# Statistics, gate columns, GpSimd sums and weight loads in an attention and gated-MLP kernel

## The chip, the core and the metric

The kernel runs on one core of one Trainium2 chip. The metric is the device time of one execution in microseconds. Before the change it is 1212.62 us, the median of 8 runs (1208.95 to 1220.15).

The core has five engines that run their own instruction queues in order: TensorE (PE, with its weight loads as PEld), VectorE (DVE), ScalarE (ACT), GpSimd (POOL) and SyncE (SP, which here only issues transfers). Transfers are also issued from ACT's and POOL's queues. [...]

## What is computed

One transformer block with conditioning, on 2048 tokens of width 1024, inputs and output in bfloat16:

```python
mod = (silu(c) @ w_mod).reshape(1, 6, 1, -1)          # sa, ca, ga, sb, cb, gb
h = layernorm(x) * (1 + ca) + sa
x = x + ga * A(h)      # 32 query heads, 4 key/value heads of 128, last 512 keys of the cache, then @ wo
h = layernorm(x) * (1 + cb) + sb
x = x + gb * ((silu(h @ w_gate) * (h @ w_up)) @ w_down)      # hidden width 3584
```

## The kernel before

**Products.** Most matrix products are made with seven block products in place of eight (class `_Seven`, `gmm`, `seven_products`). For this the two operands are cut into 2x2 blocks, and sums and differences of the blocks are needed. The sums of activations are made on VectorE. The sums of weights are made once and kept: for wq on VectorE (`sum_ops` with DVE), and for wo, w_gate, w_up and w_down on GpSimd.

**GpSimd's weight units.** One unit is 128x2048 raw weights. `units` lists 16 of wo ("o"), 28 of gate and up ("g") and 14 of w_down ("d"). For each, GpSimd issues the load into a staging slot (`unit_load`, L931), makes four sums of 128x512, each in two instructions of 128x256 (`sum_ops` with parts=2, L886, for "g"; `unit_sums`, L947, for "o" and "d"), and issues the write of the four results to DRAM (`unit_write`, L954). A sum waits for the one before it. With two slots (`OFF_ST`, at 131 and 138 KB of the arena) `unit_step` issues the next unit's load after the second of the four sums; that load waits, in GpSimd's queue, until the slot's earlier write has landed. During attention two steps are placed in every five items (`unit_tick`); in the output projection there is one slot and a step at one of the four positions of a product (`o_units`).

**Stages.** First the start: columns of w_mod for sa and ca, layernorm of the first chunk of 512 tokens, first query products. Then, for each half (two chunks of 512 tokens): attention over 64 items (`attend`; an item is one head of one chunk), output projection (`o_phase`), and later the gated MLP (`gate_up` rounds, then the last product, `f_hook`). An item of `attend` issues, in this order: `pre(i)`, half of a query product, `scores(i - 1)` with ScalarE's exponentials (L784), `pv(i - 2)` with its softmax division on VectorE (L803, L806) and a transpose from SP (L809), the other half of the query product, `tick(i)`, one background step.

**Order by hand.** The order of the program is the order of the queues. At the end of each `attend`, `start_o` and `load` issue raw blocks of wo from ACT's queue (L1148) into places that overlap GpSimd's staging slots (131 to 145 KB); the tracker `T.op` makes each wait for what last used its place. In the second half this is followed, in ACT's queue, by the last items' exponentials.

**Layernorm of the second chunk.** `load_x(1)` brings the tokens (SP, L304). From item 1 on, `ln_task(1, ..., known=False)` runs as a background task, `run_bg(2)` ahead of an item's work and one step after it: for each of four tiles the statistics (`bn_stats` L414, `bn_aggr` L418, then the reciprocal root on GpSimd, L419 and L421), the normalisation (L428) and a transpose by DMA into `hT[1]` (L451); each of these transposes waits for the one before it to land, since all write the buffers of `hT[1]`. After the four tiles come eight `modulate` operations (L433). `finish` completes the task at item 9, ahead of the first query product of the second chunk, `qproj(12)`.

**Start of the attention.** `q_raw` (L660) moves query products out of PSUM, the cast at L741 takes sa, `q_bias_mm` (L668) turns it into a bias, `q_shifted` (L673) adds it and `shift` (L678) adds sa to the first chunk. The gate columns ga come from two loads of 1 MB (`load_wga`, L571, items 2 and 3) and 64 narrow matmuls (`mod_mm` at items 7, 8 and 9). `row_task` spreads a column vector into rows with ScalarE, TensorE and VectorE, for ga and for silu(c).

**MLP weights.** `take_w` (L1426, L1427) loads for one round the raw gate block, the sums of gate, the raw up block, the sums of up, in this order, from SP's queue, two rounds ahead.

Of the kernel before, what the change touches and what calls it, by code (L numbers as in the profile page):

```python
# [131 lines left out]
def bass_adaLN_cond__sliding_block_cached__swiglu_ffn__prompt_kernel(  # L132
# [130 lines left out]
    with nc.Block() as block:  # L263

        @block.gpsimd
        def _(g):
# [177 lines left out]
            def ln_task(ch, gi, ccol, cbuf, known=True):  # L444
                dst, bufs = hT[ch % 2], B_hT[ch % 2]
                for tt in range(TPC):
                    t = ch * TPC + tt
                    if not known:
                        yield from ln_stats(t)
                    norm(t, t % 8, t % 2, half=True)  # L450
                    T.op(Q_ln[t % 2], lambda: SP.dma_start_transpose(dst[:, :, tt * P:(tt + 1) * P], nscf[t % 2]),  # L451
                         reads=[B_ns4[t % 2]], writes=bufs)
                    yield
# [272 lines left out]

            qproj_mm(4, QB0[4], 0, DT)
            q_raw(4)
            mod_sa(0)
# [116 lines left out]
            class _Seven:  # L846
# [29 lines left out]
                def sum_ops(self, st, eng, parts=1):  # L876
                    r, (s1, s2, s4) = self.raw, self.s
                    R, n = self.b_raw, HK // parts
                    for (o, a, b, op, rd, wr) in ((s1, (0, P), (HK, P), ADD, [R, self.b_s3], self.b_s[0]),
                                                  (s2, s1, (0, 0), SUB, [R, self.b_s[0]], self.b_s[1]),  # L880
                                                  (s4, (HK, 0), s2, SUB, [R, self.b_s[1], self.b_s3], self.b_s[2]),
                                                  (self.s3, (0, 0), (0, P), SUB, [R], self.b_s3)):
                        for h in range(parts):
                            x, y = [r[:, z[0] + h * n:z[0] + h * n + n, z[1]:z[1] + P] if type(z) is tuple else z[:, h * n:h * n + n, :]
                                    for z in (a, b)]
                            T.op(st, lambda: eng.tensor_tensor(o[:, h * n:h * n + n, :], x, y, op), reads=rd, writes=[wr])  # L886
                        yield
# [771 lines left out]
```

The softmax here doesn't subtract the row's maximum and nothing guards it: scores larger than these inputs give would overflow.

## Time and profile before

| what | value |
|---|---|
| median of 8 runs | 1212.62 us |
| profiled execution | 1212.46 us |
| its span | 1210.7 us |
| PE busy | 1153.2 us, 95% |
| DVE busy | 738.7 us, 61% |
| ACT busy | 527.2 us, 44% |
| POOL busy | 450.1 us, 37% |
| mean granted TensorE clock | 0.982 |
| GpSimd sums L947 and L886 | 240 and 224, mean 732 and 740 ns |

The span is the time from the first to the last instruction of the profiled execution. In the lines of a timeline, the first number is the start, the second the time from the first start to the last end of the merged instructions, and the bracket at the end gives the idle time of the engine just before and what ended it. A shape is written as partitions x elements, the output before the input.

The stages as the timeline has them: start to about 34 us; attention of the first half to about 250; output projection to about 360; attention of the second half to about 600; output projection to about 697; the MLP to the end.

### The profile page before, as it was taken

The numbers are of one execution on the slowest core, as the hardware profiler recorded it, in microseconds if no ns is written. First come the engines' busy times: TensorE is split into PE (matmuls) and PEld (weight loads), VectorE is DVE, ScalarE is ACT, GpSimd is POOL, SyncE is SP. The second block draws the span as 40 slices with busy tenths as digits, with TensorE's granted clock in tenths as the row PEclk, the third lists the DMA queues.
The fourth block names the chain that finished last, engine by engine and source line by source line (L and its number), as shares of the span: only waits on it lengthen the run. The fifth ranks groups of instructions, "written<-read, shape, count | busy, mean of one in ns | idle before, by whom it ended". The sixth has DMA issues, their size and how long they took to land.

```text
span 1210.7 us, 18388 instructions
## 1 busy us (share of the span) xinstructions
PE 1153.2 (95%) x7087; PEld 588.5 (49%) x7087; DVE 738.7 (61%) x1297; ACT 527.2 (44%) x735; POOL 450.1 (37%) x655
## 2 busy tenths in 40 slices
PE   8699999999999999996299999999999999999998
PEld 5465566654446656664144444444444444444443
DVE  4756887658676766773085767545575645454535
ACT  3466777730127777884001044545301245454110
POOL 1385588503356677777614235533400000000000
PEclk9899999999999999999599999999999999999999
DMA  9869889897948999887478577676777555544453
GB/s 327 178 181 224 172 225 215 186 209 214 228 121 176 212 194 211 197 184 197 158 191 226 174 246 239 230 256 229 248 209 203 164 187 162 188 160 152 133 172 109
DMA packets 305895, 238.72 MB, mean 197 GB/s; under 512 B 132240, under 2 KB 279696, under 8 KB 305808
## 3 DMA queue, kind: packets, MB, share of 16 engines
q1 hardware_dynamic: 234800, 121.67, 42.7%
q0 software_dynamic: 16704, 60.82, 16.1%
q10 hardware_dynamic: 54304, 55.05, 14.4%
q8 instruction: 56, 0.92, 0.3%
q14 instruction: 31, 0.25, 0.1%
HBM read 172.49 MB, written 34.60 MB: 171 GB/s over the span
## 4 chain that ended last, share of the span: by engine, by line
PE 68%; DMA 16%; POOL 11%; issue 2%; DVE 2%; ACT 1%; SPq 0%; ACTq 0%; DVEq 0%; POOLq 0%
PE ps L273 68%; POOL arena L886 9%; DMA wgu_sum<-arena 6%; DMA arena<-in_B_w_gate_dram 4%; DMA arena<-in_B_w_up_dram 3%; DMA arena<-arena 1%; POOL arena L931 1%; DMA arena<-nsc 1%; DMA arena<-in_A_wq_dram 1%; POOL arena L947 0%; POOL rstd L421 0%; DVE arena L814 0%; ACT arena L784 0%; DVE st L414 0%; DVE arena L806 0%
## 5 line engine op out<-in xcount | busy, mean ns | idle before, releaser
L273 PE MATMUL ps<-arena 128*128 128x512 f16 (+2 forms) x6782 | 1145.9, 332 | 53.2 <-ACT arena L784 33.9
L273 PEld LDWEIGHTS ps<-arena 128*128 128x128 bf16 (+1 forms) x6782 | 578.3, 98 | 613.6 <-ACT arena L784 36.4
L784 ACT ACTIVATE arena<-ps 128x1024 bf16<-128x1024 f32 x256 | 261.2, 1021 | 97.6 <-PE ps L273 49.8
L817 ACT ACTIVATE tmp<-ps 128x512 f32<-128x512 f32 x166 | 99.1, 597 | 299.1 <-PE ps L273 276.9
L947 POOL TENSOR_TENSOR arena<-arena 128x256 f16<-128x256 bf16 x240 | 174.4, 732 | 85.3 <-DMA arena<-in_B_w_down_dram 62.4
L886 POOL TENSOR_TENSOR arena<-arena 128x256 f16<-128x256 bf16 x224 | 165.7, 740 | 66.4 <-DMA arena<-in_B_w_up_dram 26.3
L814 DVE TENSOR_TENSOR arena<-ps,tmp 128x512 bf16<-128x512 f32 (+1 forms) x134 | 91.7, 684 | 51.8 <-PE ps L273 45.0
L803 DVE RECIPROCAL rl<-ps 128x4 f32<-128x4 f32 x128 | 23.0, 180 | 137.0 <-PE ps L273 136.9
L814 DVE TENSOR_TENSOR arena<-ps,nsc 128x512 f16<-128x512 f32 x84 | 57.8, 688 | 79.9 <-PE ps L273 68.2
L817 ACT ACTIVATE nsc<-ps 128x512 f32<-128x512 f32 x84 | 50.1, 597 | 95.7 <-PE ps L273 93.2
L806 DVE TENSOR_TENSOR arena<-ps,rl 128x512 f16<-128x512 f32 x128 | 88.4, 691 | 5.1 <-DMA arena<-arena 0.7
L1043 DVE TENSOR_TENSOR arena<-arena 128x2048 f16<-128x2048 f16 (+3 forms) x56 | 58.3, 1052 | 12.3 <-PE ps L273 11.7
L1493 ACT ACTIVATE arena<-arena 128x512 f16<-128x512 f16 x84 | 49.8, 624 | 30.5 <-DVE arena L814 30.5
L886 DVE TENSOR_TENSOR arena<-arena 128x512 f16<-128x512 bf16 x104 | 57.2, 550 | 1.0 <-DMA arena<-in_A_wq_dram 0.9
L814 DVE TENSOR_TENSOR tmp<-ps,tmp 128x512 f32<-128x512 f32 x32 | 22.1, 690 | 52.8 <-ACT tmp L817 43.9
L817 ACT ACTIVATE arena<-ps 128x512 f32<-128x512 f32 x16 | 9.6, 597 | 93.9 <-PE ps L273 93.9
L414 DVE BATCH_NORM_STATS2 st<-x_res 128x6 f32<-128x512 bf16 x62 | 42.3, 682 | 3.9 <-DMA x_res<-in_A_x_dram 3.4
L1510 DVE TENSOR_TENSOR arena<-ps,arena 128x512 f16<-128x512 f32 x28 | 19.4, 691 | 37.1 <-PE ps L273 37.1
L931 POOL DMA_DIRECT2D arena<-in_B_w_down_dram x14 | 11.0, 786 | 72.3 <-DMA wd_sum<-arena 44.1
L1111 DVE TENSOR_TENSOR tmp<-tmp,rowb 128x512 f32<-128x512 f32 x48 | 34.5, 720 | 1.6
L931 POOL DMA_DIRECT2D arena<-in_B_w_gate_dram x14 | 13.1, 935 | 58.7 <-PE ps L273 44.3
L1508 DVE TENSOR_TENSOR arena<-arena 128x512 f16<-128x512 f16 x84 | 34.7, 438 | 0.3
(85 smaller groups left out, 434.6 us busy)
## 6 DMA issues: line engine op xcount, KB each, us to landing
arena<-wgu_sum SPq DMA_DIRECT2D x56, 512.0 KB, 6.9
arena<-in_A_wq_dram SPq DMA_DIRECT2D x28, 512.0 KB, 5.0
wgu_sum<-arena POOLq DMA_DIRECT2D x28, 512.0 KB, 4.6
arena<-wo_sum ACTq DMA_DIRECT2D x7, 2048.0 KB, 9.3
arena<-in_B_w_gate_dram SPq DMA_DIRECT2D x28, 512.0 KB, 4.2
arena<-in_B_w_up_dram SPq DMA_DIRECT2D x28, 512.0 KB, 7.0
arena<-wd_sum ACTq DMA_DIRECT2D x8, 1792.0 KB, 8.1
arena<-in_B_w_down_dram ACTq DMA_DIRECT2D x6, 1792.0 KB, 7.3
```

The costliest lines, as they stand in the source:

```text
L273: T.op(PE, lambda: TE.matmul(out_ap, lhsT, rhs, start=start, stop=stop, skip_group_check=skip), reads=reads, writes=[bank_buf])
L414: T.op(DVE, lambda: V.bn_stats(st_[sl][:, hf * 6:hf * 6 + 6], x_res[:, t, hf * 512:hf * 512 + 512]), reads=[B_x[t]], writes=[B_st[sl]])
L784: T.op(ACT, lambda: A.activation(ex_s[es][:, 2 * kp:2 * kp + 2, :], banks2(SCB + 2 * kp), AF.Exp, scale=att_scale), writes=[PB[SCB + 2 * k ...
L806: T.op(DVE, lambda: V.tensor_tensor(o_s[os_].rearrange("p (a b) d -> p a b d", a=2), psap(PVB * 512, [[512, 2], [130, 2], [1, P]]), rlb, A ...
L814: T.op(DVE, lambda: V.tensor_tensor(out, bank(ba), other, ADD), reads=[ob2], writes=[PB[ba], ob])
L817: T.op(ACT, lambda: A.activation(dst, bank(bk), AF.Copy), writes=[PB[bk], db])
L886: T.op(st, lambda: eng.tensor_tensor(o[:, h * n:h * n + n, :], x, y, op), reads=rd, writes=[wr])
L931: T.op(Q_of[slot][0], lambda: g.dma_start(dst, src), writes=[w.b_raw, w.b_s3])
L947: T.op(POOL, lambda: g.tensor_tensor(o[:, c], a[:, c], b[:, c], SUB), reads=rd, writes=[wr])
L1043: T.op(DVE, lambda: V.tensor_tensor(o, a, b, SUB), reads=rd, writes=[sb])
L1493: T.op(ACT, lambda: A.activation(o, s_, AF.Silu), reads=[sb], writes=[ob])
L1508: T.op(DVE, lambda: V.tensor_tensor(gu[blk][:, p, :], o, s_, MULT), reads=[sb, ob], writes=[B_gu[blk][p]])
```

## The change

There are four edits.

1. Second chunk. `load_x(1)` is issued ahead of the first load of v and the second of k. The statistics of its first two tiles are made ahead of the attention, after the fifth query product has left PSUM (`stats_now`), those of the third and fourth in items 2 and 3. Each tile is normalised and transposed (`norm_turn`) in items 1 to 4, and the eight modulations come in items 7 and 8, four each, in the item's own order and no longer as a background task.
2. Gate columns. Their loads move from items 2 and 3 to 7 and 8, their matmuls from items 7, 8, 9 to 12, 13, 14. The row of silu(c) is made from item 5 on, the row of ga from item 14 on. Two blocks of the attention output are taken into use at item 14 and not 12.
3. GpSimd makes each of a unit's four sums with one instruction of 128x512.
4. `take_w` issues both raw loads ahead of both loads of sums.

```diff
             for k2 in range(DT // 2):
                 load_wsa(k2)
+            load_x(1)
             load_v(0)
             load_k(1)
-            load_x(1)
...
+            def norm_turn(ch, tt):
+                t = ch * TPC + tt
+                norm(t, t % 8, t % 2, half=True)
+                T.op(Q_ln[t % 2], lambda: SP.dma_start_transpose(hT[ch % 2][:, :, tt * P:(tt + 1) * P], nscf[t % 2]),
+                     reads=[B_ns4[t % 2]], writes=B_hT[ch % 2])
...
+            def stats_now(t):
+                for _ in ln_stats(t):
+                    pass
+
             qproj_mm(4, QB0[4], 0, DT)
             q_raw(4)
+            stats_now(TPC)
+            stats_now(TPC + 1)
             mod_sa(0)
...
-                        for h in range(parts):
...
-                            T.op(st, lambda: eng.tensor_tensor(o[:, h * n:h * n + n, :], x, y, op), reads=rd, writes=[wr])
+                        T.op(st, lambda: eng.tensor_tensor(o, a, b, op), reads=rd, writes=[wr])
...
-                    yield from w.sum_ops(POOL, g, 2)
+                    yield from w.sum_ops(POOL, g)
...
-                    for h in range(2):
-                        c = slice(256 * h, 256 * h + 256)
-                        T.op(POOL, lambda: g.tensor_tensor(o[:, c], a[:, c], b[:, c], SUB), reads=rd, writes=[wr])
+                    T.op(POOL, lambda: g.tensor_tensor(o, a, b, SUB), reads=rd, writes=[wr])
...
-                if i in (2, 3):
-                    load_wga(i - 2)
+                if i in (7, 8):
+                    load_wga(i - 7)
...
                 if i == 1:
-                    late["ln"] = ln_task(1, 0, 0, B_mode, known=False)
-                    bg.append(late["ln"])
                     scores(0)
-                if i < 9:
-                    run_bg(2)
...
-                    if i + 3 == ND:
-                        finish(late["ln"])
                     qproj(i + 3)
-                for k in {7: (0, 1, 2, 3), 8: (4, 5), 9: (6, 7)}.get(i, ()):
+                if i < 5:
+                    norm_turn(1, i - 1)
+                if 1 < i < 4:
+                    stats_now(TPC + i)
+                if i in (7, 8):
+                    for dt in range(4 * (i - 7), 4 * (i - 7) + 4):
+                        modulate(hT[1], B_hT[1], dt, 0, 0, B_mode)
+                if i == 5:
+                    bgx.append(row_task(sc_row, B_scr, sc_bf[:, :], B_sc))
+                for k in {12: (0, 1, 2), 13: (3, 4, 5), 14: (6, 7)}.get(i, ()):
                     mod_mm(wga[:, k, :], B_wga[k], k, GCOLS)
...
-                        bgx.append(row_task(sc_row, B_scr, sc_bf[:, :], B_sc))
-                if i == ND:
+                if i == ND + 2:
                     take_oT(2)
                     take_oT(3)
...
                     T.op(Q_w[sl][m][0], lambda: SP.dma_start(w.raw, src), writes=[w.b_raw])
+                for m, w in enumerate(W_of[q]):
                     T.op(Q_w[sl][m][1], lambda: SP.dma_start(w.four, wgu_sum[p, m]), reads=[B_uw[("g", p, m)]], writes=[w.b_s3] + w.b_s)
```

More of the change, by code (lines that the diff above doesn't have):

```diff
@@ L442, in ln_stats, with ln_task @@
                 yield
-            def ln_task(ch, gi, ccol, cbuf, known=True):
+            def norm_turn(ch, tt):
[3 more added lines that the diff above has]
+                     reads=[B_ns4[t % 2]], writes=B_hT[ch % 2])
+            def ln_task(ch, gi, ccol, cbuf):
                 dst, bufs = hT[ch % 2], B_hT[ch % 2]
                 for tt in range(TPC):
[L447 to L452, printed above, removed]
+                    norm_turn(ch, tt)
                     yield
@@ L874, in sums, with sum_ops @@
                         pass
[L876 to L882, printed above, removed]
[L883 to L886 removed]
+                def sum_ops(self, st, eng):
+                    r, (s1, s2, s4), s3 = self.raw, self.s, self.s3
+                    R = self.b_raw
+                    a11, a12 = r[:, 0:HK, 0:P], r[:, HK:DT, 0:P]
+                    a21, a22 = r[:, 0:HK, P:2 * P], r[:, HK:DT, P:2 * P]
+                    for (o, a, b, op, rd, wr) in ((s1, a21, a22, ADD, [R, self.b_s3], self.b_s[0]),
+                                                  (s2, s1, a11, SUB, [R, self.b_s[0]], self.b_s[1]),
+                                                  (s4, a12, s2, SUB, [R, self.b_s[1], self.b_s3], self.b_s[2]),
+                                                  (s3, a11, a21, SUB, [R], self.b_s3)):
+                        T.op(st, lambda: eng.tensor_tensor(o, a, b, op), reads=rd, writes=[wr])
                         yield
```

## The prediction

> **What bounds the kernel now.** I read the page's busy shares, then who TensorE waits for, then the timeline around its longest wait, then the first 70 us. TensorE is busy 1153.2 of 1210.7 us, so at most 57 us can go without less work. Its waits, columns total us, times, longest us:
>
> ```profile
> PE ps L273 <- ACT arena L784: 33.9, 4, 32.4
> PE ps L273 <- DVE arena L806: 5.6, 1, 5.6
> PE ps L273 <- DVE bq L668: 3.6, 2, 2.5
> ```
>
> One wait, 32.4 us, is over half of what is idle. It lies where the second attention pass ends:
>
> ```profile
> 558.57 7.60 PE L273 MATMUL ps<-arena 128*128 128x512 bf16 x58 [0.51 <-ACT arena L784]
> 584.50 0.58 POOL L954 DMA_DIRECT2D wgu_sum<-arena  x1 [0.30 <-POOL arena L886]
> 585.99 5.75 POOL L947 TENSOR_TENSOR arena<-arena 128x256 f16<-128x256 bf16 x8
> 587.55 8.81 ACTq L1148 DMA_DIRECT2D arena<-in_A_wo_dram  x3
> 592.04 0.65 POOL L954 DMA_DIRECT2D wd_sum<-arena  x1 [0.30 <-POOL arena L947]
> 596.41 2.14 ACT L784 ACTIVATE arena<-ps 128x1024 bf16<-128x1024 f32 x2 [35.87 <-POOL rstd L419]
> 598.61 13.66 PE L273 MATMUL ps<-arena 128*128 128x129 bf16 x63 [32.45 <-ACT arena L784]
> ```
>
> ScalarE holds a softmax exponential that TensorE needs, but ahead of it in ScalarE's queue are loads of wo (L1148) into the staging slots in which GpSimd forms weight sums. The first is issued when the write of 584.50 has landed (3.0 us), the last when that of 592.04 has (595.04). So GpSimd's weight units end 29 us after TensorE stops (566.2), and TensorE's end moves with them. The label "rstd" is merely what GpSimd ran last. The chain of waits agrees: from 280.0 to 595 it holds GpSimd sums, their writes and loads; before 280.0 it holds TensorE, whose products free the first slot (GpSimd's load of 280.00 waited 44.31 us for them). A unit's cycle in the two-slot stage:
>
> ```profile
> 450.44 2.90 POOL L886 TENSOR_TENSOR arena<-arena 128x256 f16<-128x256 bf16 x4 [1.70 <-DMA arena<-in_B_w_gate_dram]
> 455.82 0.94 POOL L931 DMA_DIRECT2D arena<-in_B_w_up_dram  x1 [2.49 <-DMA wgu_sum<-arena]
> 456.78 2.99 POOL L886 TENSOR_TENSOR arena<-arena 128x256 f16<-128x256 bf16 x4
> 460.08 0.58 POOL L954 DMA_DIRECT2D wgu_sum<-arena  x1 [0.31 <-POOL arena L886]
> 460.76 2.90 POOL L886 TENSOR_TENSOR arena<-arena 128x256 f16<-128x256 bf16 x4
> ```
>
> Four sums, wait for the other slot's write, load, four sums, write. Here both DMA waits show, so only one of the two halves counts in a cycle. The mean cycle from 387.87 to 584.50 is 9.83 us, of which 7.9 is GpSimd's own.
>
> The front, where the second chunk's layernorm is made:
>
> ```profile
> 26.87 0.69 DVE L660 COPY arena<-ps 128x512 f32<-128x512 f32 x1 [4.19 <-PE ps L273]
> 27.48 0.15 DVE L741 CAST mod_bf<-ps 128x8 bf16<-128x8 f32 x1
> 31.77 1.41 DVE L414 BATCH_NORM_STATS2 st<-x_res 128x6 f32<-128x512 bf16 x2
> 33.60 5.34 PE L273 MATMUL ps<-arena 128*128 128x512 f16 x28 [2.52 <-DVE bq L668]
> 55.94 2.82 DVE L433 TENSOR_SCALAR arena<-arena,gain,mod_bf 128x512 f16<-128x512 f16 x4 [5.18 <-DMA arena<-nsc]
> 60.23 4.78 PE L273 MATMUL ps<-arena 128*128 128x129 bf16 x24 [5.63 <-DVE arena L806]
> ```
>
> VectorE stands 5.18 us at the modulation (L433) until the last of four serial transposes lands; item 4's softmax division (L806) is behind it, and TensorE behind that.
>
> [...] Here 128x256 takes 0.669 us at the median (0.655 least); no 128x512 is shown. [...] VectorE's L886 sums take 0.412 to 0.910 us, GpSimd's up to 1.729. [...] Here v's first group, k's second and x's second chunk land at 26.2, 26.6 and 29.3 us, in order of issue.
>
> **The change, part by part.** The sum is made against the profiled execution: 1212.46 us, span 1210.7 and 1.8 around it; the median of eight is 1212.62.
>
> *GpSimd sums whole.* Eight instructions a unit become four. A pair now takes 2 x 0.745 = 1.49 us start to start. [...] Saved 0.20 a pair, 0.40 a half unit. Lower end: no fixed part, 1.34 + 0.07, 0.08 a pair[...]. Upper: if all of the 128x1 scalar operation's 0.22 us (L419) is fixed, 512 takes 1.12 and 0.30 is saved.
> How many halves count: I replayed GpSimd's own instructions from 280 to 595 with the landing time of each load and write as it was. In the single-slot stage (five units, 288 to 373) both halves count, 10; of the following 21 two-slot units one, 21; in the final units, where TensorE stands and DMA is fast (cycles 8.4 to 8.8), both, 5 more. 36 halves x 0.40 = 14.4 us. Bounds: 36 x 0.16 = 6 and 36 x 0.60 = 22. Further, from 288 to 342 the eight sums took 9.88, 7.23 and 8.18 us instead of 6.0, because VectorE's big subtractions alternate with them: 7.3 us lost; with half as many instructions perhaps half the waits: +3. DMA is busy 0.96 to 1.01 in 375 to 500; units 4% closer together may lengthen landings: 0.1 us on some 26 cycles, -2. Sum -15 on the end of the units, and as 15 is under 32.4, all of it is TensorE's. What is late next is still the last unit's write.
> Cost: VectorE is held up to 0.55 us longer. GpSimd sums run in 107.8 of 193 us (372 to 565), so a two-input operation meets one in 0.56 of cases, halfway through: +0.15 us on 128 operations (104 sums L886, 24 L594), 20 us of VectorE, spread over windows where it idles 13 to 32%. I take 2 us of it as TensorE's.
>
> *Statistics early.* x's second chunk is issued two places earlier: minus 0.9 us, landing 28.4 (26 to 29.3); v and k land some 2.7 later, needed after 36, so nothing (without this cover 2.7). VectorE reaches the new statistics after the fifth evacuation at 22.7 and stands until 28.4. Behind it stand the seventh evacuation, the cast of mod_bf, bq and the shifts; TensorE's bias products wait for the cast. Two tiles cost 2 x 1.57: VectorE at 31.5, cast done 32.3 (now 27.6): TensorE idles 4.5 us, new. But the tile of statistics that stood ahead of bq (1.57) is gone: bq's second pair comes at 36.5 (now 33.4), and item 2's products start 3.1 us late. Then the two short waits (1.13 and 0.69) vanish: item 5 begins at 48.5 (now 47.1), item 7 at 54.4 (52.8).
>
> *Modulation at items 7 and 8.* The four transposes stay serial, 37 to about 55, with some 4.5 us each. The modulation now stands behind item 4's division, so TensorE runs on: 0.86 scores, 1.1 values, 1.73 projection, 0.86, 1.1, and the first projection of the second chunk starts at 60.1 to 61.6 (DVE's last four modulations 1.1 to 2.8 us after 58.8). Now that is 65.26 + 0.86 + 1.1 = 67.2. Gain 6; the half-clock matmuls after 60.23 (0.43 us apart) are in it.
>
> *Gate columns.* Two loads (SP issues of 0.43 and 0.58 us) move from 36.7 and 43.2 to items 7 and 8, past transposes L451 and L809; the transpose of 45.16, beside such a load, took 5.8 us against 3.3 to 3.9 before. Their 64 narrow matmuls (1.9 us) mostly filled idle time; at items 12 to 14 they are on the path: +1.2. The load has 14 us and took 7.1; uncovered it would cost under 2. The row of c earlier: 1.2 us of VectorE and 1.3 of ScalarE beside transposes; if uncovered 1.2. oT taken two items later: no instruction.
>
> Front: 6 - 1.2 = 4.8, less 0.8 for the late x at the worst half: -4 (from +2, x at 29.3 and slow transposes, to -7). It passes on whole, since GpSimd's chain starts from TensorE at 280.
>
> *Raw weights first.* A round lasts 12.1 us (713.92, 726.00, 738.09), loads are issued two rounds ahead and land in 4 to 7: nothing. Uncovered, at the first round, 1 to 2.
>
> Sum: 1212.5 - 15 + 2 - 4 = 1195.5; I say 1195.
>
> **Rivals.** (1) *DMA sets the units' pace:* landings lengthen by what the sums save (DMA share about 1.0; many cycles wait for a write), so only the front and the single-slot stage gain: 1212 - 4 - 3 = 1205. Against it: the waits are latencies, and 9.83 us a unit is no fixed rate (8.4 at the end). (2) *The longer lock makes VectorE the bound, slower:* in 150 to 175 VectorE is busy 21.8 of 25 us, and each softmax division queues behind a sum. It decides from the point where an item's VectorE work passes TensorE's 3.5 us: if half of the 128 operations meet it with the full 0.55, 35 us come in, 19 go: 1228. Against it: in 125 to 235 VectorE idles 21.9 us just ahead of the divisions. (3) *The change doesn't move the end:* sums near 1.34 us each and x landing late: 1210. (4) *The stall goes nearly whole* (upper prices): 1183.
>
> **Numbers.** Forecast 0.62, with its own range 1186 to 1204; rival 1 0.14, 2 0.12, 3 0.07, 4 0.05. The measurement tells 0.5% (6 us) from no change. Faster: forecast, 4 and most of 1: 0.77; same: 3 and the rest of 1: 0.11; slower 0.12. Range 1184 to 1212: it leaves out rival 2 and part of 4.
>
> **What would show it.** After: 128x512 on GpSimd at 1.1 to 1.3 us; TensorE's wait at the end of attention 13 to 22 us, ended by L1148 again; a new wait of 3 to 5 us near 28 behind bn_stats; none at 55 to 60; L594 and L886 on VectorE somewhat longer. Wrong if 128x512 is over 1.4 us, if the cycle stays at 9.8, or if TensorE shows many waits for L806 between 125 and 235.

## The result and the profile after

The changed kernel takes 1199.37 us (median of 11 runs, 1192.7 to 1207.66), the kernel before 1213.2 (median of 32, 1203.73 to 1221.86). The ratio is 0.9882, its 95% interval 0.9856 to 0.9909: about 14 us faster, where 17.5 were forecast. The profiled execution of after is one of its shortest: 1192.99 us, span 1191.2. A twelfth run of after (1210.82 us) fell in a slower state that some executions show, and such runs are left out of all ratios here; the profiled executions of chained and of gate columns early, below, are of that kind.

In the lines of after, L784 has become L791, L806 L813, L814 L821, L886 L892, L931 L937, L947 L951, L954 L958, L1148 L1152, L594 L595, L741 L748 and L451 L447.

The waits of TensorE in after, largest first (total us, times, longest us):

```profile
PE ps L273 <- DVE arena L821: 10.1, 13, 3.5
PE ps L273 <- DVE mod_bf L748: 4.4, 1, 4.4
PE ps L273 <- issue: 3.8, 1, 3.8
PE ps L273 <- DVE arena L813: 3.0, 5, 1.0
...
PE ps L273 <- ACT arena L791: 1.7, 4, 0.5
```

The 32.4 us for ScalarE are gone from this execution. In their place stand 13 waits for L821, an operation on VectorE that moves a product (in the attention a query product) out of PSUM; in the first attention and projection before, where it is L814, it made two waits of 2.6 us together. The timeline at the end of the second attention shows why the long wait went:

```profile
560.34 4.79 POOL L951 TENSOR_TENSOR arena<-arena 128x512 f16<-128x512 bf16 x4
565.42 0.65 POOL L958 DMA_DIRECT2D wd_sum<-arena  x1 [0.30 <-POOL arena L951]
569.61 32.75 PE L273 MATMUL ps<-arena 128*128 128x512 bf16 x185 [0.51 <-ACT arena L791]
570.67 4.23 ACTq L1152 DMA_DIRECT2D arena<-in_A_wo_dram  x3
```

The last unit's sums are four instructions and the write is issued at 565.42, not 592.04. ScalarE passes its three loads while TensorE still multiplies.

To see where the difference arises I read from each trace the start of the n-th of the 256 exponentials, and split the profiled span there. The fourth piece runs from the 253rd to the 255th; it holds the wait for the loads of wo, and takes 4 to 5 us where there is none.

| us | before | after | gain |
|---|---|---|---|
| start to 17th (front) | 69.8 | 64.0 | +5.8 |
| 17th to 129th (first attention, projection) | 287.1 | 300.8 | -13.7 |
| 129th to 253rd (second attention) | 201.5 | 204.7 | -3.2 |
| 253rd to 255th | 38.0 | 5.4 | +32.6 |
| from there to the end | 614.3 | 616.3 | -2.0 |
| span | 1210.7 | 1191.2 | +19.5 |

So this execution gained 38 us in two places and gave 19 back in the others. Three parts of that need an explanation: 32.6 us at the wait where 15 were forecast, the 17 us that the two attention passes lost, and the front.

### The profile page after: what moved, and what is told of

It is laid out like the page before. It is cut to its first block, busy times and chain, and to the rows that moved or that the text cites. A ratio compares the mean times of both kernels' runs of the same rounds, so it can differ in the third digit from the quotient of the medians.

```text
span 1191.2 us, 18157 instructions
## 1 busy us (share of the span) xinstructions
PE 1157.0 (97%) x7087; PEld 586.3 (49%) x7087; DVE 774.0 (65%) x1297; ACT 527.3 (44%) x735; POOL 387.8 (33%) x423
## 4 chain that ended last, share of the span: by engine, by line
PE 88%; DVE 8%; issue 1%; SPq 1%; DMA 1%; ACT 1%; ACTq 0%; DVEq 0%
PE ps L273 88%; DVE arena L892 1%; DMA x_res<-in_A_x_dram 1%; DVE arena L821 1%; DVE arena L813 1%; DVE arena L595 1%; DVE st L414 1%; DVE x_res L1116 1%; DVE arena L433 0%; SPq L342 0%; DVE arena L836 0%; ACT arena L791 0%; DVE arena L834 0%; DVE tmp L1115 0%; DVE tmp L821 0%
## 5 line engine op out<-in xcount | busy, mean ns | idle before, releaser
L273 PE MATMUL ps<-arena 128*128 128x512 f16 (+2 forms) x6782 | 1149.8, 332 | 26.2 <-DVE arena L821 10.1
L791 ACT ACTIVATE arena<-ps 128x1024 bf16<-128x1024 f32 x256 | 261.2, 1022 | 65.3 <-PE ps L273 53.5
L951 POOL TENSOR_TENSOR arena<-arena 128x512 f16<-128x512 bf16 x120 | 140.7, 1184 | 91.7 <-DMA arena<-in_B_w_down_dram 68.2
L892 POOL TENSOR_TENSOR arena<-arena 128x512 f16<-128x512 bf16 x112 | 136.9, 1222 | 64.2 <-DMA arena<-in_B_w_up_dram 33.1
L821 DVE TENSOR_TENSOR arena<-ps,tmp 128x512 bf16<-128x512 f32 (+1 forms) x134 | 91.5, 683 | 44.8 <-PE ps L273 41.4
L821 DVE TENSOR_TENSOR arena<-ps,nsc 128x512 f16<-128x512 f32 x84 | 57.8, 688 | 78.4 <-PE ps L273 66.8
L813 DVE TENSOR_TENSOR arena<-ps,rl 128x512 f16<-128x512 f32 x128 | 88.4, 691 | 5.4 <-DMA arena<-arena 0.8
L892 DVE TENSOR_TENSOR arena<-arena 128x512 f16<-128x512 bf16 x104 | 85.2, 819 | 0.1
L821 DVE TENSOR_TENSOR tmp<-ps,tmp 128x512 f32<-128x512 f32 x32 | 22.0, 688 | 41.6 <-ACT tmp L824 33.2
L595 DVE SCALAR_TENSOR_TENSOR arena<-arena 128x1024 bf16<-128x1024 bf16 x24 | 39.3, 1636 | 0.0
L1515 DVE TENSOR_TENSOR arena<-arena 128x512 f16<-128x512 f16 x84 | 37.7, 473 | 0.3
L428 DVE TENSOR_SCALAR nsc<-x_res,mv,rstd 128x1024 f16<-128x1024 bf16 (+1 forms) x30 | 17.3, 578 | 29.6 <-DMA arena<-nsc 29.5
L937 POOL DMA_DIRECT2D arena<-in_B_w_gate_dram x14 | 13.1, 935 | 69.6 <-PE ps L273 48.8
```

The source lines that it names most:

```text
L273: T.op(PE, lambda: TE.matmul(out_ap, lhsT, rhs, start=start, stop=stop, skip_group_check=skip), reads=reads, writes=[bank_buf])
L595: T.op(DVE, lambda: V.scalar_tensor_tensor(mt[n % 2], mt[n % 2], 1.0, sc_row, op0=ALU.mult, op1=ALU.mult, accum_out=mcol[:, n:n + 1]), rea ...
L791: T.op(ACT, lambda: A.activation(ex_s[es][:, 2 * kp:2 * kp + 2, :], banks2(SCB + 2 * kp), AF.Exp, scale=att_scale), writes=[PB[SCB + 2 * k ...
L813: T.op(DVE, lambda: V.tensor_tensor(o_s[os_].rearrange("p (a b) d -> p a b d", a=2), psap(PVB * 512, [[512, 2], [130, 2], [1, P]]), rlb, A ...
L821: T.op(DVE, lambda: V.tensor_tensor(out, bank(ba), other, ADD), reads=[ob2], writes=[PB[ba], ob])
L892: T.op(st, lambda: eng.tensor_tensor(o, a, b, op), reads=rd, writes=[wr])
```

## The experiments

The theory after the result: (a) whole sums shorten GpSimd's chain and so the wait at its end; (b) whole sums hold VectorE longer, and that is what the attention lost; (c) the front gains by itself, by one of its edits. The main rival to (b): denser GpSimd work slows the transfers, and VectorE's longer instructions are only seen beside it. Each kernel's ratio is against the kernel before, on the same chip. The pieces of each profiled span, in the cut of the table above (one execution each; sums only and wo loads late have the front of before, and their fronts differ by 2.5 us):

| us | front | first attention | second | 253rd to 255th | span |
|---|---|---|---|---|---|
| sums only | 70.2 | 296.5 | 206.9 | 16.9 | 1204.3 |
| front only | 62.8 | 287.1 | 201.3 | 36.8 | 1201.0 |
| loads as before | 64.1 | 304.4 | 203.2 | 14.9 | 1201.4 |
| chained | 63.2 | 294.4 | 203.5 | 24.3 | 1203.8 |
| no reads | 62.0 | 286.7 | 201.1 | 18.2 | 1185.2 |
| wo in halves | 64.3 | 291.7 | 202.3 | 14.1 | 1184.1 |
| wo loads late | 67.7 | 286.1 | 201.6 | 4.3 | 1200.5 |
| halves and late loads | 63.1 | 292.5 | 205.2 | 4.3 | 1179.6 |
| later statistics | 64.4 | 302.4 | 204.4 | 18.8 | 1207.5 |
| gate columns early | 69.9 | 287.9 | 206.5 | 15.4 | 1193.3 |
| quarters | 61.0 | 305.5 | 201.3 | 70.5 | 1268.2 |

### The parts one at a time

**Sums only.** The kernel before with edit 3 alone:

```diff
-                    yield from w.sum_ops(POOL, g, 2)
+                    yield from w.sum_ops(POOL, g)
...
-                    for h in range(2):
-                        c = slice(256 * h, 256 * h + 256)
-                        T.op(POOL, lambda: g.tensor_tensor(o[:, c], a[:, c], b[:, c], SUB), reads=rd, writes=[wr])
+                    T.op(POOL, lambda: g.tensor_tensor(o, a, b, SUB), reads=rd, writes=[wr])
```

> The kernel before with whole GpSimd sums alone. Theory: the sums carry both the gain and the loss. The 32 us wait at the end of the second attention goes or falls under 5 us, VectorE's own L886-type sums rise from a mean of 0.55 to about 0.8 us, TensorE loses about 15 us in the two attentions and the projection between; total 1203 to 1206, that is the change without its front (4 to 5 us). Rival (the front makes the loss by moving work into the attention): the attention is as fast as before and the total is 1190 or less. Rival (the front makes the gain): 1213.

Measured: 1203.05 us against 1214.62, ratio 0.9893 (0.9855 to 0.9931). The wait at the end is 10.6 us, 21.8 shorter, though not under the 5 expected. The first attention is 9.4 us longer, the second 5.4, and the front 0.4. Edit 3 alone thus makes the large gain and most of the loss.

**Front only.** The change with the sums in halves and `take_w` in the old order (edits 1 and 2 alone):

> The change with sums in halves and the loads as before, so statistics, modulation and gate columns alone. Theory: the front is 4 to 5 us shorter at item 9 and this passes to the end whole, since GpSimd's units start from TensorE's progress: 1208 to 1209, with the wait before the second projection still 30 to 34 us and no loss in the attention. Rival (the front is swallowed by that wait): 1213. Rival (the front causes the attention's loss): the second chunk's items 26 to 48 lose 8 us, 1215 to 1220.

Measured: 1208.57 us against 1214.62, ratio 0.995 (0.993 to 0.9971), 6 us. The attention passes take 287.1 and 201.3 us, as before, and the wait is 31.2 us. So the front's gain passes on whole: it starts GpSimd's chain earlier (at 273.3 us and not 280.0) and leaves the wait at its end as it was. The two parts alone add up to 11.6 + 6.0 = 17.6 us, against 14 together, but the intervals are about as wide as that gap.

**Loads as before.** The change with edit 4 undone:

```diff
                     T.op(Q_w[sl][m][0], lambda: SP.dma_start(w.raw, src), writes=[w.b_raw])
-                for m, w in enumerate(W_of[q]):
```

> The change with the MLP weight loads in their old order. Theory: nothing, 1199, since each is issued two rounds (24 us) ahead and lands in 4 to 7. Rival: the new order costs or saves at the first round, where TensorE waits for nothing that the profile shows for 3.8 us (2.2 before): 1 to 2 us.

Measured: 1201.57 us, ratio 0.9881 (0.9842 to 0.992), that of the change. Edit 4 does nothing that can be told from these runs; the interval is 9 us wide.

### What the attention lost

VectorE's sums in after, the first attention and projection, then the second attention (least, median and longest in ns):

```profile
L892 DVE TENSOR_TENSOR arena<-arena x48: 405/418/3247, 106.7 to 358.9; 128x512 f16<-128x512 bf16 x36, 128x512 f16<-128x512 f16 x12
L892 DVE TENSOR_TENSOR arena<-arena x56: 412/610/2097, 376.6 to 560.4; 128x512 f16<-128x512 bf16 x42, 128x512 f16<-128x512 f16 x14
```

The same two groups before:

```profile
L886 DVE TENSOR_TENSOR arena<-arena x48: 412/420/910, 111.3 to 349.6; 128x512 f16<-128x512 bf16 x36, 128x512 f16<-128x512 f16 x12
L886 DVE TENSOR_TENSOR arena<-arena x56: 412/417/909, 368.6 to 549.7; 128x512 f16<-128x512 bf16 x42, 128x512 f16<-128x512 f16 x14
```

The medians tell little; the tail tells it. None of these sums took 1 us before, and now the longest takes 3.25. What such a one meets is seen in the timeline of after (start, then how long the merged instructions lasted):

```profile
142.02 2.27 POOL L951 TENSOR_TENSOR arena<-arena 128x512 f16<-128x512 bf16 x2
142.05 3.33 DVE L595 SCALAR_TENSOR_TENSOR arena<-arena 128x1024 bf16<-128x1024 bf16 x1
...
160.22 0.82 POOL L937 DMA_DIRECT2D arena<-in_A_wo_dram  x1 [1.67 <-DMA wo_sum<-arena]
160.38 3.25 DVE L892 TENSOR_TENSOR arena<-arena 128x512 f16<-128x512 bf16 x1
161.07 2.26 POOL L951 TENSOR_TENSOR arena<-arena 128x512 f16<-128x512 bf16 x2
163.63 0.58 POOL L958 DMA_DIRECT2D wo_sum<-arena  x1 [0.30 <-POOL arena L951]
165.09 3.09 PE L273 MATMUL ps<-arena 128*128 128x512 f16 x7 [3.49 <-DVE arena L821]
```

At 142.05 VectorE's instruction, 1.2 us when undisturbed, begins just after the first of two GpSimd sums has begun and is held until both are over (144.29), then does its work. At 160.38 it begins while GpSimd issues a transfer, and is held through that and both sums. Behind it in VectorE's queue is L821, and TensorE waits 3.49 us for L821. The granted clock of TensorE then reads 0.5 for 3.4 us from 164.6 on, so the long wait costs about 1.5 us more in slower multiplication (an estimate from these times); in before the clock is 1.00 throughout the first attention. VectorE's instruction came in between the two sums in neither case. In the wo and w_down units the fourth sum doesn't read the third's result, so it waits for nothing, unlike what I wrote of all sums in the section on the kernel before; here it started 0.05 us before the third had ended. In halves all others waited for the one before (both halves write what one buffer stands for), with a gap of 0.08 us, and the longest of VectorE's sums was 0.91 us; only the fourth sum's first half followed without one, so that two halves of 0.67 us were the longest stretch. In the gate and up units the fourth sum writes over what the third reads, so it waits anyway: that fits the second attention, which meets hardly any but these and has 2.1 us at the longest.

**Chained.** The change, but the fourth sum is made to wait for the third in every unit, by naming its buffer as read:

```diff
-                                                  (s3, a11, a21, SUB, [R], self.b_s3)):
+                                                  (s3, a11, a21, SUB, [R, self.b_s[2]], self.b_s3)):
...
-                                          (e[2], b21, e[1], [R, w.b_s[1]], w.b_s[2]), (rf[:, 1536:2048], b22, b12, [R], w.b_s3)):
+                                          (e[2], b21, e[1], [R, w.b_s[1]], w.b_s[2]), (rf[:, 1536:2048], b22, b12, [R, w.b_s[2]], w.b_s3)):
```

> The change, with the fourth sum of each unit made to wait for the third. Theory: in the changed kernel the third and fourth sums run back to back (2.27 us for two of 1.16) and VectorE's two-input instruction waits for both (2.45 to 3.33 us seen); with a gap between them the longest such wait is one sum, so VectorE's sums fall from a mean of 0.82 to 0.6 or 0.7 with none over 2 us, TensorE's waits in the attention fall by half, and the total falls by 4 to 8 us to about 1193, if the units (some 0.1 us longer each) still end ahead of TensorE. Rival (it is the length of a single sum that matters): no change, 1199. Rival (the units end later and the wait returns): over 1203.

Measured: 1194.07 us, ratio 0.981 (0.9763 to 0.9857). The longest of VectorE's sums is now 2.1 us and not 3.25, and the first attention 6.4 us shorter than in after. TensorE's waits in it fall from 13.4 to 9.0 us and not by half, and the mean of the sums is 759 ns, above the 600 to 700 expected: most of the hold is that of one whole sum and stays. Its profiled run is one of its longest (1205.62), with 16.1 us of the wait at the end; the first attention doesn't rest on that wait, and the granted clock in it is 1.00, as in before.

**No reads.** To separate the hold from all else, GpSimd's sums are left out and each is replaced by two memsets of 128x512, which read nothing and take 0.53 us each; the loads and writes stay. The weight sums are zero in this kernel, so its time, and no result, is read:

```diff
-                    T.op(POOL, lambda: g.tensor_tensor(o, a, b, SUB), reads=rd, writes=[wr])
+                    for _ in range(2):
+                        T.op(POOL, lambda: g.memset(o, 0.0), reads=rd, writes=[wr])
```

> The change with each GpSimd sum left out and two memsets of its output put in its place (the weight sums are then zero, so the output is not the reference's): GpSimd writes as long as before but reads nothing from SBUF. Theory: VectorE's two-input instructions are no longer held, their mean is 0.42 us with none over 1, and the 13 us that the first attention lost come back: 285 to 288 us from exponential 16 to 128 instead of 301; the wait before the second projection is under 10 us; 1180 to 1188. Rival (the loss comes from GpSimd's transfers or from the moved gate columns): the stretch stays at 298 to 301.

Measured once: 1187.05 us; the profiled execution has, for VectorE's sums,

```profile
L896 DVE TENSOR_TENSOR arena<-arena x104: 415/415/426, 104.7 to 541.1; 128x512 f16<-128x512 bf16 x78, 128x512 f16<-128x512 f16 x26
```

No sum is held, and the attention passes take 286.7 and 201.1 us: all 17 us are back, with the same transfers and with GpSimd busy for 351 us (388 in after). This decides against the rival: GpSimd's reading, and not its transfers, is what the loss needs. A wait of 12.7 us at the end stays, more than the 10 expected.

**wo in halves.** The change, with two half instructions in the wo units alone, the ones in which the fourth sum waits for nothing and which the first attention meets most:

```diff
-                    T.op(POOL, lambda: g.tensor_tensor(o, a, b, SUB), reads=rd, writes=[wr])
+                    for h in range(2 if units[k][0] == "o" else 1):
+                        n = 256 if units[k][0] == "o" else 512
+                        c = slice(n * h, n * h + n)
+                        T.op(POOL, lambda: g.tensor_tensor(o[:, c], a[:, c], b[:, c], SUB), reads=rd, writes=[wr])
```

> The change with the sums of wo's 16 units, which are made in the first attention, in halves, and those of gate, up and down whole. Theory: the first attention runs as before the change (287 us from exponential 16 to 128, 301 in the change), nothing waits for wo's units there, and the second stage keeps the shorter chain; since GpSimd's chain for the second half starts from TensorE's progress, the 10 us or so pass to the end as far as the wait does not grow: 1188 to 1192. Rival (TensorE arrives earlier and waits the longer): 1198.

Measured: 1190.48 us, ratio 0.9831 (0.9781 to 0.9881). The first attention takes 291.7 us, 9.1 of its 13.7 back and not all of it as expected; the waits for L821 are 6.6 us and not 10.1. A finer cut of that piece, by the same exponentials, shows what is left:

| us | 17th to 33rd | 33rd to 121st | 121st to 129th |
|---|---|---|---|
| before | 28.9 | 144.6 | 113.6 |
| sums only | 28.9 | 153.4 | 114.3 |
| after | 30.0 | 154.3 | 116.5 |
| chained | 30.0 | 149.7 | 114.7 |
| wo in halves | 30.0 | 145.4 | 116.2 |
| no reads | 30.0 | 143.7 | 113.0 |
| gate columns early | 28.9 | 144.9 | 114.2 |

The 1.1 us in the first column is in every kernel with edit 2, no reads among them, and in none without: the matmuls of the gate columns at items 12 to 14, which were forecast at 1.2, and no hold. The second column is the attention itself, in which GpSimd first makes wo's units; there the change loses 9.7 us and wo in halves 0.8. The third is the projection, in which gate and up units stay whole in wo in halves, and it loses 2.6 as the change loses 2.9.

**Quarters.** The other end of the dose: four instructions of 128x128 for each sum.

```diff
-                    yield from w.sum_ops(POOL, g)
+                    yield from w.sum_ops(POOL, g, 4)
...
+                    for h in range(4):
+                        c = slice(128 * h, 128 * h + 128)
```

> The change with each GpSimd sum in four instructions of 128x128: the other end of the same dose. From 0.669 us for 128x256 and 1.16 for 128x512 the slope is 1.92 ns an element and 0.18 fixed, so 128x128 takes 0.42 us, 0.50 start to start, 2.0 a sum against 1.49 in halves and 1.24 whole. Theory: VectorE's two-input sums are held less than in halves (mean 0.45 to 0.55 us), the first attention is as fast as with halves (287 us from exponential 16 to 128 of 256), and the wait before the second projection grows to 60 to 75 us (36 half units x 1.0 us on top of 31): about 1245. Rival (the units' pace is set by DMA): the wait stays near 32, 1210.

Measured once: 1270.0 us. In the page, GpSimd's and VectorE's sums (total us, mean ns), then from the waits the longest:

```profile
L954 POOL TENSOR_TENSOR arena<-arena 128x128 f16<-128x128 bf16 x480 | 229.4, 480 | 103.7 <-DMA arena<-in_B_w_down_dram 67.2
L893 DVE TENSOR_TENSOR arena<-arena 128x512 f16<-128x512 bf16 x104 | 49.3, 474 | 0.4 <-DMA arena<-in_A_wq_dram 0.2
```

```profile
PE ps L273 <- ACT arena L791: 81.4, 6, 64.9
```

VectorE's mean falls with the size of GpSimd's instruction: 819 ns at 512 columns, 550 before at 256, 474 at 128. The chain's wait goes the other way: 64.9 us, a second one of 14.5 us at the end of the first attention, and one of 11.4 us, ended at 947.6, for sums of w_down. The loss was 25 us larger than expected, and I had counted on neither of those two. From the 33rd to the 121st exponential the kernel takes 144.2 us, no more than before. The size of GpSimd's instruction thus trades one wait against the other.

### The wait at the end

**wo loads late.** If the wait is only the order of ScalarE's queue, then the loads behind the last exponentials must make it vanish. The kernel before, with one number changed:

```diff
-                    if i == hi - 1:
+                    if i == hi:
                         wo0[sc][0](0, (1,))
                         wo0[sc][0](1)
```

> The kernel before, with one edit of its own: the second group of wo loads, which ScalarE issues at the end of each attention, placed one item later, behind the last exponentials in ScalarE's queue. Theory: what TensorE waits 32 us for is the exponential that stands behind these loads, and the loads wait for GpSimd's last units. With the exponentials ahead, TensorE goes on for 6 to 8 us (two value products, early wo products) and then waits for wo itself, which still comes only with the units' end near 592: the wait shrinks by 6 to 10 us, is ended by a load of wo and not by L784, and the total is 1203 to 1207. Rival (the exponentials are late for another reason): no change, 1213.

Measured: 1201.47 us, ratio 0.991 (0.988 to 0.9939). The timeline of this kernel:

```profile
555.56 10.23 PE L273 MATMUL ps<-arena 128*128 128x512 bf16 x82 [0.51 <-ACT arena L784]
583.67 9.06 ACTq L1148 DMA_DIRECT2D arena<-in_A_wo_dram  x3
586.55 10.77 PE L273 MATMUL ps<-arena 128*128 128x512 bf16 x36 [20.76 <-DMA arena<-in_A_wo_dram]
```

The exponentials pass, TensorE works on until the first product that needs these blocks of wo, and then waits 20.8 us for the load itself. So 11 of the 32 us were the queue's order, a little more than the 6 to 10 expected, and the rest is the chain of units.

**Halves and late loads.** The same number changed in the kernel with wo in halves:

> The change with wo's sums in halves and the same group of wo loads one item later. Theory: of the wait that was left (8.5 us in the profile) 6 to 8 us are covered by work that does not need wo: 1182 to 1186. Rival: 1190, as without it.

Measured: 1186.41 us, ratio 0.9773 (0.9737 to 0.9808). This is the fastest version whose runs lie close together, 13 us below the change by the medians, and just above the 1182 to 1186 expected. The wait at the end of the attention is gone from its waits of TensorE, the largest of which are:

```profile
PE ps L273 <- DVE arena L821: 7.5, 10, 1.4
PE ps L273 <- DVE mod_bf L748: 3.7, 1, 3.7
PE ps L273 <- issue: 3.7, 1, 3.7
```

### The front

**Later statistics.** The change, with the first two tiles' statistics moved from ahead of the attention into item 1, behind bq, so that the wait of 4.4 us for the cast of mod_bf can't arise:

```diff
-            stats_now(TPC)
-            stats_now(TPC + 1)
...
+                if i == 1:
+                    stats_now(TPC)
                 if i < 5:
                     norm_turn(1, i - 1)
-                if 1 < i < 4:
+                if i < 4:
                     stats_now(TPC + i)
```

> The change with the statistics of the first two tiles of the second chunk moved from ahead of the attention into item 1, behind bq. Theory: the wait of 4.4 us for the cast of mod_bf goes, item 2's products start about 5 us earlier, of which 2 to 4 us are left at item 9 because VectorE has two tiles more to do between; 1196 or 1197. Rival (VectorE's extra work in items 1 to 4 delays the softmax divisions by as much): 1199 to 1201.

Measured: 1200.13 us, ratio 0.991 (0.9884 to 0.9937): no gain over the change. The cast is over at 27.4 us, the first exponential starts at 29.8 instead of 35.8, but the ninth at 49.1 and in after at 49.3. The 4.4 us are hidden by item 8: what the early items win, TensorE waits for again (3.1 us for VectorE between 36 and 52 us, 0.3 in after).

**Gate columns early.** The kernel with wo in halves, with the loads of the gate columns back at items 2 and 3, their matmuls at 7 to 9 and the rows as before, so that of edits 1 and 2 the statistics and the modulation remain:

```diff
-                if i in (7, 8):
-                    load_wga(i - 7)
+                if i in (2, 3):
+                    load_wga(i - 2)
...
-                for k in {12: (0, 1, 2), 13: (3, 4, 5), 14: (6, 7)}.get(i, ()):
+                for k in {7: (0, 1, 2, 3), 8: (4, 5), 9: (6, 7)}.get(i, ()):
```

> The change with wo's sums in halves and the gate columns where they were: loads in items 2 and 3, matmuls in items 7 to 9, rows and the taking of oT as before. It tells what that edit is worth, since the other parts are known. As I priced it: 1.2 us of matmuls come off the path, and the serial transposes of the second chunk, beside 2 MB of loads, end 2 to 5 us later, some of which the modulation waits for: 1190 to 1193, that is the same within what can be told. Rival (the transposes end late enough to stop TensorE as in the kernel before): 1194 to 1197 with a wait of 3 to 6 us near 60.

Its runs lie between 1175.98 and 1204.38 us, so the time decides nothing. In the profiled execution the front takes 69.9 us, as in the kernel before.

```profile
44.65 0.59 SPq L572 DMA_DIRECT2D arena<-in_w_mod_dram  x1
46.15 1.23 SPq L447 DMA_TRANSPOSE arena<-nsc  x1
57.44 1.30 SPq L447 DMA_TRANSPOSE arena<-nsc  x1
60.74 2.60 DVE L433 TENSOR_SCALAR arena<-arena,gain,mod_bf 128x512 f16<-128x512 f16 x4 [6.11 <-DMA arena<-nsc]
64.22 4.78 PE L273 MATMUL ps<-arena 128*128 128x129 bf16 x24 [5.36 <-DVE arena L813]
```

The transpose issued behind the load of 1 MB lands 11.2 us later (the next one is issued at 57.44, when it has), the modulation waits for it and TensorE for the division behind that. In the kernel with wo in halves the same transpose, at 45.27, has no such load beside it and takes 3.3 us. But this order doesn't always cost 11.2 us. Before, sums only and wo loads late issue the same transpose behind the same load, and there it took 5.9, 5.8 and 3.9 us. With 5.9, an estimate, 5.3 of the 6.11 us that the modulation waited would not have come. And at the end of the projection this execution is only 1.8 us behind that of wo in halves (the first two pieces of the table). So the profile shows what a late transpose does to TensorE, not that the move of the gate columns prevents it. In after the modulations no longer wait:

```profile
28.70 1.42 DVE L414 BATCH_NORM_STATS2 st<-x_res 128x6 f32<-128x512 bf16 x2 [5.92 <-DMA x_res<-in_A_x_dram]
32.37 0.15 DVE L748 CAST mod_bf<-ps 128x8 bf16<-128x8 f32 x1
32.58 0.59 PE L273 MATMUL ps<-mod_bf,arena 128*128 128x1 bf16 x16 [4.39 <-DVE mod_bf L748]
58.05 1.39 DVE L433 TENSOR_SCALAR arena<-arena,gain,mod_bf 128x512 f16<-128x512 f16 x4
60.32 6.05 PE L273 MATMUL ps<-arena 128*128 128x129 bf16 x49 [1.00 <-DVE arena L813]
```

## Why the prediction held, point by point

**The total.** The forecast of 17.5 us and the 14 measured agree, but errors of opposite sign are in it, so part of the agreement is luck, and one step failed.

**GpSimd sums whole: right in kind, with two terms too small that work against each other.** The bracket for one instruction held: 128x512 takes 1.162 us at the median, between the bounds of 1.12 and 1.34, which came from the 0.669 us of 128x256 and the 0.22 of L419 in the trace of before. The 0.20 us saved a pair, that is 1.49 - 0.20 = 1.29 us start to start for a whole sum, was an estimate of mine that the trace of before did not show. The first term that was too small is the own time saved on the chain from the load of 280 us to the last write: 54 half units x 0.40 and 3 for fewer waits between sums would be 24.6 us, of which the replay let 17.4 through. GpSimd's sums on that chain went from 160.0 to 132.0 us, and the idle time between them that isn't DMA's from 13.9 to 5.2: 36.7 us, half again as much as 24.6. A whole sum was priced well: 132.0 + 5.2 over 108 sums is 1.27 us start to start, against 1.29. The pair of halves wasn't: 160.0 + 13.9 over 108 is 1.61 us and not 1.49, since I took the median, and the mean of the halves lies above it (741 ns to 669) where VectorE holds one. With half as many instructions there are half as many chances of that. The second is what goes back to DMA: 7.2 us by the replay, in which a shorter sum waits the longer for a write that lands when it did, and 2 for longer landings. The waits of GpSimd for DMA on the chain, before:

```profile
POOL arena L931 <- DMA wgu_sum<-arena: 38.4, 16, 7.3
POOL arena L886 <- DMA arena<-in_B_w_gate_dram: 25.7, 9, 7.7
POOL arena L886 <- DMA arena<-in_B_w_up_dram: 22.7, 10, 6.1
```

and after:

```profile
POOL arena L937 <- DMA wgu_sum<-arena: 40.2, 18, 8.3
POOL arena L892 <- DMA arena<-in_B_w_up_dram: 29.2, 12, 7.0
POOL arena L892 <- DMA arena<-in_B_w_gate_dram: 23.2, 12, 5.1
```

The sum of the three is 86.8 before and 92.6 after, so 5.8 us came back to DMA in this execution. In the seven other profiled kernels with whole gate and up sums of real weights it is 95.8 to 110.5 us, 9 to 24 more than before (with the sums in halves it is 80.8 to 86.8, in three). With the mean of all eight, 102.1, 15.3 of the 36.7 us are given back. Part of it is that the writes of gate and up sums land later: from issue to landing they took 4.5 to 4.8 us on average in the three with halves and 4.9 to 5.5 in the eight with whole sums, some 0.45 us more on 26 writes, while GpSimd's loads took 5.7 to 5.9 and 5.5 to 5.9. So rival 1's mechanism, transfers that take up part of what the sums save, is real at some 40% of the saving.

The length of the chain, from the load that waits for TensorE to the issue of the last write, tells the same: 312.7 us before (310.9 and 312.1 in the two others with halves), 281.3 in after, but 289.1 to 302.4 in the seven others with whole sums, on average 16 us less than with halves. That is close to the forecast 15; the 31 of after's profiled execution are the best of eight. How much of the wait is left changes with it: 7.6 us with the loads as before, 10.6 with sums only, 13.3 with later statistics, 16.1 chained. The forecast of 13 to 22 us for this wait fits the last two; the profiled execution of after had none. What is left depends on the chain's start too: it begins when TensorE reaches the projection, at 284.8 us in after and 288.9 in sums only. So what the first attention loses delays the chain and passes on whole, while a loss in the second is hidden as long as a wait is left at its end. What in the transfers' order makes them longer or shorter from one execution to the next was not settled.

**The step that failed: "+0.15 us on 128 operations (104 sums L886, 24 L594), 20 us of VectorE [...] I take 2 us of it as TensorE's".** Measured on VectorE, from the groups by stage: sums and L595 together took 16.1 us more in the first attention and projection (25.8 to 40.5, 16.7 to 18.1) and 17.3 in the second (31.3 to 44.7, 17.5 to 21.4). That is 33 us, 0.26 an operation. In the second attention 3.2 us of it reached TensorE, no great miss against the 2 for both. In the first the step failed: of the 13.7 us lost there 1.1 are the gate columns', and 12.6 reached TensorE, with no more VectorE time behind them.

One difference is the length of the single hold. I had capped it at 0.55 us more, one whole sum against one half (an estimate; measured, it is 1.162 - 0.669 = 0.49), because the step took it that each instruction of GpSimd lets the next of VectorE in. Two sums with no semaphore between them didn't, and VectorE's longest sum grew by 2.3 us (0.91 to 3.25). Breaking up the pairs alone (chained) leaves 5.1 of the attention's 9.7 us (33rd to 121st), halving wo's sums leaves 0.8, and taking away GpSimd's reads leaves nothing. So the hold is the cause: rival 2's mechanism, at half of its price of 35. Nearly all of the attention's part comes with wo's units, about half of it from the pairs and half from the length of the whole sum. The projection's 2.9 us go with the reads too; in the kernels with whole gate and up sums they are 0.6 to 2.9, and what sets how much was not settled. Nor was why chained still loses 5.1 us in the first attention, where its second, with like holds, loses 2.0.

Beside GpSimd's sums, which read two tiles, VectorE's longest sum took 3.25 us in after; beside its memsets, which read nothing, 0.426 us (no reads). The sign that I had named for the longer hold, waits for the operation at VectorE between 125 and 235 us, came, under another line (L821, not L806).

**Statistics, modulation, gate columns: right in size, its cause open.** -4 us was forecast; front only measured -6. The 1.2 us for the matmuls of the gate columns came (1.1). The new wait came as priced (4.5 forecast, 4.4 measured), the stall at the division fell from 5.6 to 1.0. Of two terms, one was wrong and one is not shown in what it rests on. The wait for the cast was put against the gain, and costs nothing at item 8 (later statistics). And the gain was put down to the modulation's place in the order, with the loads of the gate columns only as something moved; in the profiled execution of gate columns early that place didn't help, because a transpose beside those loads took 11.2 us. Since the same transpose took 3.9 to 5.9 us in three other executions, and the times of that kernel decide nothing, which of edits 1 and 2 carries the gain is not shown.

**Raw weights first: nothing, as forecast** (loads as before).

**Not settled.** TensorE's wait put down to "issue" late in the second output projection was 2.2 us before and 3.8 in after, 0.9 in wo in halves and 4.7 in later statistics. It is most of the 2.0 us lost in the last piece. The granted clock of 0.5 takes about as much from both last pieces: it lasts 6.8 us from 659.5 on in after, and in before it goes on for 7.2 us after the 255th exponential. No experiment was aimed at this.

## What to carry to other kernels

Where the instructions of one engine hold up another's, as GpSimd's sums did VectorE's here, price the longest unbroken stretch of the holder, and set it against the slack of one step of the work behind the waiting engine; a mean over all instructions hides it (here 0.82 us, with 3.25 the longest). Longer instructions on the off-path engine were worth having here where its chain sets an end (21.8 us of wait in sums only), and worth cutting, or chaining by a semaphore, where the other engine feeds the bound one (9.1 and 6.4 us of the first attention). A queue in which a transfer with a late condition stands ahead of work that is ready (11 of the 32 us here) is worth a look before the chain that makes the condition late is sped up.

## What the runs showed of the hardware

A GpSimd sum of two tiles took 0.669 us for 128x256 (before) and 1.162 for 128x512 (after), at the median; the line through these two, an estimate, has 1.9 ns an element of a row and 0.18 us fixed and would give 0.42 for 128x128, where quarters has a mean of 0.48. Two independent ones in a row overlapped by 0.05 us in after, and VectorE's sum L892 and its L595, which read two tiles each, took 3.25 and 3.33 us beside them in place of 0.42 and 1.2; with a semaphore wait between the two (chained) VectorE's longest sum was 2.1 us. A transfer's issue by GpSimd (0.82 us) with sums right behind it added to the hold (at 160.38 and 170.16 in after); at 355.69, with no sum right behind, VectorE's sum took 0.424 us during such an issue. The memset of 128x512 in float16 took 0.53 us (no reads), and beside it the longest of VectorE's 104 sums took 0.426. The third transpose of the second chunk, issued behind the second load of 1 MB, took 3.9, 5.8, 5.9 and 11.2 us in four profiled executions, and 3.3 in three without such a load. While TensorE stood for 32.45 us in before, its granted clock went to 0.5 at 569.5, 3.3 us after it stopped, and stayed there until 603.6, 5 us after it went on. ScalarE stood idle for 35.87 us in before, with its last two exponentials behind three transfers that waited for their places; with the same transfers behind those exponentials (wo loads late) it stood idle for 2.16 us ahead of them.
